# One change to a long-convolution, gate and ELU-MLP kernel: the filter's four steps taken from four groups in each slot, and two subtractions of the first part moved to GpSimd

## The chip, the cores and the metric

The kernel runs on one core of a Trainium2 chip. The metric is the device time of one execution in microseconds (us). Three runs of the kernel before gave 3637.33 us as their median (3637.32 to 3637.77). About 0.2% (7 us) is what a measurement of this kernel can tell from no change.

## The reference

Two stages, all in float32. The first gates two inputs, convolves the product along the sequence (12480 long, by a Fourier transform of twice that length) with a filter that a small MLP makes from position embeddings, and gates the result again. The second is an MLP with ELU.

```python
B, S, D = 4, 12480, 128                       # x, v: (4, 12480, 128); pos_emb: (12480, 64)
h_mlp  = np.maximum(pos_emb @ w1, 0.0) @ w2   # w1 64x64, w2 64x128
h_filt = h_mlp * np.exp(-0.01 * pos)[:, None]
u  = x * v
Uf = np.fft.rfft(u, n=2 * S, axis=1)
Hf = np.fft.rfft(h_filt, n=2 * S, axis=0)
y  = np.fft.irfft(Uf * Hf[None], n=2 * S, axis=1)[:, :S]
a  = (x * y).reshape(B * S, D)
h  = a @ w_in                                 # w_in 128x2048, float64 in DRAM
g  = np.where(h > 0, h, np.exp(np.minimum(h, 0)) - 1)
out = g @ w_out                               # w_out 2048x128, float64 in DRAM
```

## The kernel before

The transform is split in two: 104 x 60 positions per half of the sequence. Stage 1 does transforms of length 104 as matmuls, stage 2 the ones of length 60, the product with the filter's spectrum and the first half of the way back. The rest of the way back and the MLP run block by block. A float32 operand of a large matmul is split in a rounded high part (`_h`) and a rest (`_l`, the subtraction), and `mm3` multiplies them in three matmuls (lines 53, 54, 55).

The program has three parts. The **first part** is stage 1 of batch 0 together with the filter and the conversion of the MLP's weights (`first=True`). The second is stage 2 of batch 0. The third is the MLP of all batches, with the stages of batches 1 to 3 beside it. Only the first part is touched. Its order is written out by hand: each engine executes its instructions in the order in which the code issues them, and SyncE issues all the large DMAs in that order.

The first part runs over 15 groups `g` of 4 columns of 60. For each group x and v are loaded (`xt`, `vt`), gated (`vt = xt * vt`, line 102, on GpSimd from group 2 on), split (`u_h` on ScalarE, line 110, `u_l` on VectorE, line 111) and transformed in four pieces `i`, each an `mm3` of 512 columns into `aps`. Two pieces are a **slot** `q = 2g + r`, the pieces of a slot being `w = 0` and `w = 1`; there are 30 slots. The output `a_sb` is copied from PSUM by VectorE for `w = 0` (line 153) and by ScalarE for `w = 1`, and stored to `a_d`.

In slot q the filter's group q + 1 (of 30) is also made, in four steps: `step(q+1, 0)` transposes four tiles of `pos` into `pt` (line 217) and ScalarE copies them to `pt_sb`; `step(q+1, 1)` multiplies by `w1` into `rp` (line 223), and ScalarE writes the ReLU `r_sb` (line 225); `step(q+1, 2)` multiplies by `w2` into `hps` (line 231), VectorE multiplies by the window into `h_sb` (line 234), ScalarE writes `h_h`, and VectorE the rest `h_l` (line 242); `transform(q)` then multiplies the group made in the slot before by the transform matrix into `Hps` (12 matmuls of 256 columns), ScalarE and VectorE write `hsb` from it (VectorE at line 256), and it is stored to `h_d`. `pt`, `rp` and `hps` share one pool of two PSUM banks.

In each of the first 16 slots one of 16 chunks of the MLP's weights is also converted from float64: ten VectorE instructions (`weights`, lines 290 to 307), and in the slot after that `split_w`, which copies the high part (`wi_h`, `wo_h`, ScalarE) and subtracts on GpSimd (`wi_l`, `wo_l`, line 318).

Of the kernel before, what the change touches and what calls it, by code (L numbers as in the profile page):

```python
# [38 lines left out]
def fftconv_gate_elu_mlp_kernel(ctx: ExitStack, tc: tile.TileContext, x, v, pos_emb, w1, w2,  # L39
# [41 lines left out]
    def stage1(st, h, ps_pool, ps_tag, first):  # L81
# [22 lines left out]
        def split(g):  # L104
            if g >= NG:
                return
            vt = ld.pop(g)[1]
            u_h = up.tile([N1, 2, G, D], F32R, tag="u_h", name="u_h")
            u_l = up.tile([N1, 2, G, D], F32R, tag="u_l", name="u_l")
            copy(u_h, vt)  # L110
            nc.vector.tensor_tensor(out=u_l, in0=vt, in1=u_h, op=ALU.subtract)
            us[g] = (u_h, u_l)

        def store():
# [4 lines left out]

        if first:  # L120
            filt = Filter(st)
            for g in range(4):
                filt.load(g)
                if g < 3:
                    load(g)
                filt.load_w(g)
            gate(0)
            gate(1)
            for q in range(3):
                filt.step(0, q)  # L130
        else:
            load(0)
            load(1)
            gate(0)
            gate(1)
        split(0)
        for g in range(NG):
            if first:
                gate(g + 2)
            u_h, u_l = us.pop(g)  # L140
            for i in range(4):
                r, w = divmod(i, 2)
                f = FWD[w][r]
                if w == 0:
                    a_sb = ap.tile([N1, G, Z, 2, D], F32 if first else F32R, tag="a_sb", name="a_sb")
                if first:
                    q = 2 * g + r
                    filt.step(q + 1, 2 * w)
                ps = ps_pool.tile([N1, 512], F32, tag=ps_tag, name="aps")
                mm3(ps, dft_h[:, f, :], dft_l[:, f, :], u_h[:, w], u_l[:, w])  # L150
                src = ps.rearrange("p (n d) -> p n d", n=G)
                if first and w == 0:
                    nc.vector.tensor_copy(out=a_sb[:, :, 0, w], in_=src)
                else:
                    copy(a_sb[:, :, 0, w], src)
                if not first:
                    nc.vector.tensor_tensor(out=a_sb[:, :, 1, w], in0=src, in1=a_sb[:, :, 0, w], op=ALU.subtract)
                if first:
                    if w == 0:
                        filt.step(q + 1, 1)  # L160
                        filt.load(q + 4)
                        filt.load_w(q + 4)
                    else:
                        filt.transform(q)
                        filt.weights(q)
                        filt.split_w(q - 1)
# [12 lines left out]
        if first:
            filt.flush()  # L180


    class Filter:
# [2 lines left out]

        def __init__(self, st):
            c1 = st.enter_context(tc.tile_pool(name="c1", bufs=1))
            self.pp = st.enter_context(tc.tile_pool(name="pp", bufs=5))
            self.hp = st.enter_context(tc.tile_pool(name="hp", bufs=1))  # L190
            self.wl = st.enter_context(tc.tile_pool(name="wl", bufs=1))
            self.psh = st.enter_context(tc.tile_pool(name="psh", bufs=2, space=PS))
            self.psH = st.enter_context(tc.tile_pool(name="psH", bufs=1, space=PS))
            self.w1 = c1.tile([64, 64], F32, name="w1_sb")
            self.w2 = c1.tile([64, D], F32, name="w2_sb")
            self.win = c1.tile([N1, 2, N2], F32, name="win_sb")
            nc.scalar.dma_start(out=self.w1, in_=w1)
# [11 lines left out]
        def step(self, g, q):  # L209
# [2 lines left out]
            hp, psh = self.hp, self.psh  # L212
            if q == 0:
                p = self.pos.pop(g)
                pt = psh.tile([64, 2 * GF, N1], F32, tag="h", name="pt")
                for n in range(2 * GF):
                    nc.tensor.transpose(out=pt[:, n, :], in_=p[:, n // GF, n % GF, :], identity=id_sb[:N1, :N1])
                pt_sb = hp.tile([64, 2 * GF, N1], F32, tag="pt_sb", name="pt_sb")
                copy(pt_sb, pt)
                self.t[g] = pt_sb  # L220
            elif q == 1:
                rp = psh.tile([64, 2 * GF, N1], F32, tag="h", name="rp")
                nc.tensor.matmul(out=rp, lhsT=self.w1, rhs=self.t[g], start=True, stop=True)
                r_sb = hp.tile([64, 2 * GF, N1], F32, tag="r_sb", name="r_sb")
                nc.scalar.activation(out=r_sb, in_=rp, func=ACTF.Relu)
                self.t[g] = r_sb
            elif q == 2:
                r_sb = self.t.pop(g)
                hps = psh.tile([N1, 2, GF, D], F32, tag="h", name="hps")
                for n in range(2 * GF):  # L230
                    nc.tensor.matmul(out=hps[:, n // GF, n % GF, :], lhsT=r_sb[:, n, :], rhs=self.w2,
                                     start=True, stop=True)
                h_sb = hp.tile([N1, 2, GF, D], F32, tag="h_sb", name="h_sb")
                nc.vector.tensor_tensor(
                    out=h_sb, in0=hps,
                    in1=self.win[:, :, g * GF:(g + 1) * GF].rearrange("p w (n o) -> p w n o", o=1).to_broadcast([N1, 2, GF, D]),
                    op=ALU.mult)
                h_h = hp.tile([N1, 2, GF * D], F32R, tag="h_h", name="h_h", bufs=2)
                h_l = hp.tile([N1, 2, GF * D], F32R, tag="h_l", name="h_l", bufs=2)
                hv = h_sb.rearrange("p w n d -> p w (n d)")  # L240
                copy(h_h, hv)
                nc.vector.tensor_tensor(out=h_l, in0=hv, in1=h_h, op=ALU.subtract)
                self.hs[g] = (h_h, h_l)

        def transform(self, g):
# [21 lines left out]
        def load_w(self, i):  # L267
# [1 line left out]
            if i >= self.NW:  # L269
                return  # L270
            m, c = divmod(i, DFF // WC)
            z = self.wl.tile([128, WC, 2], U32, tag="z", name="z", bufs=5)
# [385 lines left out]
    with ExitStack() as st:  # L658
# [3 lines left out]
        nc.scalar.dma_start(out=id_sb, in_=ident)  # L662
        copy(dft_h, dft_sb)
        nc.vector.tensor_tensor(out=dft_l, in0=dft_sb, in1=dft_h, op=ALU.subtract)
        psa = st.enter_context(tc.tile_pool(name="psa", bufs=4, space=PS))
        for _ in stage1(st, 0, psa, "a", True):
            pass
    with ExitStack() as st:
# [68 lines left out]
```

## Time and profile before

| what | value |
|---|---|
| median of 3 runs | 3637.33 us |
| the profiled execution: time / span of its trace | 3646.31 us / 3644.5 us |
| TensorE busy, whole span | 3434.0 us (94%) |
| VectorE / ScalarE / GpSimd busy, whole span | 3136.5 / 2418.3 / 2276.2 us |
| mean granted TensorE clock, whole span | 0.967 |
| first part, end of the first `Hps` to end of the last | 29.4 to 271.9 us |
| in that stretch: TensorE / VectorE / ScalarE / GpSimd busy | 211.2 / 143.1 / 94.2 / 75.7 of 242.6 us |

The profiled execution is 9 us (0.25%) longer than the median of the runs. Busy times are those of the hardware profiler; a matmul's end is modelled and lies some tenths of a microsecond behind the start of the one that follows, so starts are compared with starts. The granted clock is a share of 2.4 GHz; 0.50 is 1.2 GHz.

### The profile page before, as it was taken

To read this page: it belongs to the slowest core of one execution; us is meant where nothing else is said; L and a number is where in the kernel's file an instruction comes from. 1 tells how busy PE (TensorE), PEld (TensorE's weight loads), DVE (VectorE), ACT (ScalarE), POOL (GpSimd) and SP (SyncE) were. 2 spreads that over 40 slices of the span, in tenths; PEclk is the share of its full clock that TensorE was granted. 3 is DMA by queue.
4 is the path that set the end of the run, shared out by engine and by line. 5 is a ranking of instruction groups with operands and counts; after the bars stand their busy time and mean duration, and the time that the engine had idled before them with its cause. 6 is when DMAs were issued, how large, how long until landed. Compare 5 with 4: busy or idle time off the path is not lost.

```text
span 3644.5 us, 53113 instructions
## 1 busy us (share of the span) xinstructions
PE 3434.0 (94%) x18444; PEld 3158.4 (87%) x18444; DVE 3136.5 (86%) x3941; ACT 2418.3 (66%) x3290; POOL 2276.2 (62%) x1578
## 2 busy tenths in 40 slices
PE   7887878989999999989999999989999999999999
PEld 5666767879998998879999998879999999999998
DVE  5647988989999988989999988979999988888887
ACT  3334546866666677866666677866666677777776
POOL 3406875857777765557766756657666655655555
PEclk8769998999999999999999999999999999999999
DMA  6648886767777735778888846778888832222220
GB/s 186 185 127 241 267 242 194 222 181 201 203 205 208 201 109 165 242 202 220 238 221 229 227 114 185 241 199 225 233 228 232 237 88 60 59 66 60 69 59 24
DMA packets 383995, 646.29 MB, mean 177 GB/s; under 512 B 24679, under 2 KB 170439, under 8 KB 374367
## 3 DMA queue, kind: packets, MB, share of 16 engines
q1 hardware_dynamic: 383305, 642.73, 62.4%
q8 instruction: 146, 2.39, 0.3%
q14 instruction: 123, 1.00, 0.1%
q10 hardware_dynamic: 421, 0.16, 0.0%
HBM read 412.76 MB, written 230.03 MB: 176 GB/s over the span
## 4 chain that ended last, share of the span: by engine, by line
PE 76%; DVE 8%; ACT 4%; DMA 4%; issue 4%; POOL 3%; SPq 0%; POOLq 0%; DVEq 0%; ACTq 0%
PE fps L53 9%; PE fps L55 9%; PE fps L54 9%; PE ops L53 9%; PE ops L54 9%; PE ops L55 8%; PE bps L439 4%; DVE g_l L567 2%; PE xps L53 2%; PE xps L54 2%; PE xps L55 2%; PE yps L53 2%; PE yps L54 2%; PE yps L55 2%; PE otp L589 1%
## 5 line engine op out<-in xcount | busy, mean ns | idle before, releaser
L561 POOL CAST g_h<-g 128x832 fp32r<-128x832 f32 x960 | 1232.5, 1286 | 1051.3 <-DVE g L558 1050.5
L551 ACT ACTIVATE n<-fps 128x832 f32<-128x832 f32 x960 | 831.9, 867 | 723.1 <-PE fps L55 704.2
L558 DVE SCALAR_TENSOR_TENSOR g<-n,fps 128x832 f32<-128x832 f32 x960 | 975.9, 1017 | 258.5 <-ACT n L552 253.0
L567 DVE TENSOR_TENSOR g_l<-g,g_h 128x832 fp32r<-128x832 f32 x960 | 1097.7, 1143 | 9.3 <-POOL g_h L561 9.3
L552 ACT ACTIVATE n<-n 128x832 f32<-128x832 f32 x960 | 864.4, 900 | 30.5
L53 PE MATMUL fps<-t_h,wi_h 128*128 128x416 f32 x1920 | 716.4, 373 | 0.7 <-ACT t_h L58 0.7
L54 PE MATMUL ops<-g_l,wo_h 128*128 128x416 f32 x1920 | 680.9, 355 | 23.6 <-DVE g_l L567 23.2
L53 PE MATMUL ops<-g_h,wo_h 128*128 128x416 f32 x1920 | 680.4, 354 | 4.7
L55 PE MATMUL fps<-t_h,wi_l 128*128 128x416 f32 x1920 | 677.0, 353 | 0.0
L54 PE MATMUL fps<-t_l,wi_h 128*128 128x416 f32 x1920 | 676.7, 352 | 0.0
L55 PE MATMUL ops<-g_h,wo_l 128*128 128x416 f32 x1920 | 675.1, 352 | 0.0
L420 POOL TENSOR_TENSOR p<-p 120x768 f32<-120x768 f32 x204 | 480.9, 2357 | 69.2 <-DVE p L414 49.3
L54 PEld LDWEIGHTS ops<-g_l,wo_h 128*128 128x128 f32 x1920 | 362.3, 189 | 45.8 <-DVE g_l L567 41.1
L53 PEld LDWEIGHTS fps<-t_h,wi_h 128*128 128x128 f32 x1920 | 364.2, 190 | 21.3 <-ACT t_h L58 1.0
L53 PEld LDWEIGHTS ops<-g_h,wo_h 128*128 128x128 f32 x1920 | 361.6, 188 | 20.0 <-issue 17.5
L54 PEld LDWEIGHTS fps<-t_l,wi_h 128*128 128x128 f32 x1920 | 365.8, 191 | 15.0 <-DVE t_l L540 0.3
L55 PEld LDWEIGHTS fps<-t_h,wi_l 128*128 128x128 f32 x1920 | 362.7, 189 | 2.8
L55 PEld LDWEIGHTS ops<-g_h,wo_l 128*128 128x128 f32 x1920 | 361.5, 188 | 3.4
L412 DVE TENSOR_TENSOR p<-xps,f 120x512 f32<-120x512 f32 x416 | 283.4, 681 | 24.9 <-DMA f<-f_d 14.7
L421 POOL TENSOR_TENSOR p<-p 120x256 f32<-120x256 f32 x204 | 246.0, 1206 | 16.0
L439 PE MATMUL bps<-p,t 120*120 120x256 f32 x832 | 219.1, 385 | 31.5 <-POOL p L421 26.6
L347 DVE TENSOR_TENSOR tl<-t,th 120x360 fp32r<-120x360 f32 x208 | 202.1, 971 | 44.9 <-ACT th L58 31.4
(95 smaller groups left out, 4979.0 us busy)
## 6 DMA issues: line engine op xcount, KB each, us to landing
a_d<-a_sb SPq DMA_DIRECT2D x90, 832.0 KB
al<-a_d SPq DMA_DIRECT2D x156, 480.0 KB
f<-f_d SPq DMA_DIRECT2D x312, 240.0 KB
b_d<-b_sb SPq DMA_DIRECT2D x156, 480.0 KB
b<-b_d SPq DMA_DIRECT2D x90, 832.0 KB
t<-in_tab_dram SPq DMA_DIRECT2D x208, 281.2 KB
xt<-in_x_dram SPq DMA_DIRECT2D x60, 416.0 KB
vt<-in_v_dram SPq DMA_DIRECT2D x60, 416.0 KB
```

Source lines behind the costliest of these rows:

```text
L53: nc.tensor.matmul(out=ps, lhsT=hi, rhs=bh, start=start, stop=False)
L54: nc.tensor.matmul(out=ps, lhsT=hi, rhs=bl, start=False, stop=False)
L55: nc.tensor.matmul(out=ps, lhsT=lo, rhs=bh, start=False, stop=stop)
L412: nc.vector.tensor_tensor(out=p[:, :, :2], in0=ps[:, :, 0:1, :].to_broadcast([RI, TG, 2, D]), in1=f[:, :, r], op=ALU.mult)
L420: e.tensor_tensor(out=q, in0=q, in1=p, op=ALU.add)
L421: e.tensor_tensor(out=q[:, :, 1], in0=q[:, :, 1], in1=q[:, :, 2], op=ALU.add)
L439: nc.tensor.matmul(out=ps[:, o], lhsT=t[:, o, 3 * N2:], rhs=y[:, o, :2], start=True, stop=True)
L551: nc.scalar.activation(out=n, in_=ps[:, :, :NT], func=ACTF.Relu, scale=-1.0)
L552: nc.scalar.activation(out=n, in_=n, func=ACTF.Exp, scale=-1.0)
L558: nc.vector.scalar_tensor_tensor(out=g, in0=n, scalar=-1.0, in1=ps[:, :, :NT], op0=ALU.add, op1=ALU.max)
L561: nc.gpsimd.tensor_copy(out=g_h, in_=g)
L567: nc.vector.tensor_tensor(out=g_l, in0=g, in1=g_h, op=ALU.subtract)
```

## The change

In slot q the filter's steps are now taken from four different groups: `step(q+3, 0)`, then the first piece's `aps`, `step(q+1, 2)`, `step(q+2, 1)`, the second piece's `aps` and `transform(q)`. What a step needs was issued in an earlier slot. Before the first slot the first steps of the groups 0 to 2 are issued. `pt`, `rp` and `hps` have a PSUM bank each, `aps` has three banks instead of four, and the SBUF tiles between the steps have two buffers. The conversion of the weights' chunks is spread: one in each of the slots 0, 1 and 2 and then one in every second slot up to 28. The subtractions `u_l` (from group 1 on) and `h_l` go from VectorE to GpSimd.

```diff
@@ stage1, split and the start
-            nc.vector.tensor_tensor(out=u_l, in0=vt, in1=u_h, op=ALU.subtract)
+            e = nc.gpsimd if first and g else nc.vector
+            e.tensor_tensor(out=u_l, in0=vt, in1=u_h, op=ALU.subtract)
...
-            for g in range(4):
+            for g in range(5):
                 filt.load(g)
                 if g < 3:
                     load(g)
                 filt.load_w(g)
             gate(0)
+            for q in range(3):
+                for i in range(3 - q):
+                    filt.step(i, q)
             gate(1)
-            for q in range(3):
-                filt.step(0, q)
@@ stage1, the slots
                 if first:
                     q = 2 * g + r
-                    filt.step(q + 1, 2 * w)
+                    filt.step(q + 3 - w, w)
...
                     if w == 0:
-                        filt.step(q + 1, 1)
-                        filt.load(q + 4)
-                        filt.load_w(q + 4)
+                        filt.step(q + 1, 2)
+                        filt.load(q + 5)
                     else:
                         filt.transform(q)
-                        filt.weights(q)
-                        filt.split_w(q - 1)
+                        if q % 2 == 0 or q == 1:
+                            c = (q + 1) // 2 + (q > 1)
+                            filt.load_w(c + 5)
+                            filt.weights(c)
+                            filt.split_w(c - 1)
@@ Filter
-            self.psh = st.enter_context(tc.tile_pool(name="psh", bufs=2, space=PS))
+            self.psh = st.enter_context(tc.tile_pool(name="psh", bufs=1, space=PS))
...
-                pt = psh.tile([64, 2 * GF, N1], F32, tag="h", name="pt")
+                pt = psh.tile([64, 2 * GF, N1], F32, tag="t", name="pt")
...
-                rp = psh.tile([64, 2 * GF, N1], F32, tag="h", name="rp")
+                rp = psh.tile([64, 2 * GF, N1], F32, tag="r", name="rp")
...
-                nc.vector.tensor_tensor(out=h_l, in0=hv, in1=h_h, op=ALU.subtract)
+                nc.gpsimd.tensor_tensor(out=h_l, in0=hv, in1=h_h, op=ALU.subtract)
@@ the first part's PSUM
-        psa = st.enter_context(tc.tile_pool(name="psa", bufs=4, space=PS))
+        psa = st.enter_context(tc.tile_pool(name="psa", bufs=3, space=PS))
```

Left out here: `pt_sb`, `r_sb` and `h_sb` get two buffers, `pos` and `z` six instead of five, and the last `split_w` follows the last slot.

TensorE, from one `transform` to the next (one slot, `Hps` left out), the rows of before with - and of the change with +:

```order
-L217 MATMUL pt<-id_sb,pos 64x104 x4
-L53 MATMUL aps<-u_h,dft_h 104x512
-L54 MATMUL aps<-u_l,dft_h 104x512
-L55 MATMUL aps<-u_h,dft_l 104x512
-L223 MATMUL rp<-pt_sb,w_sb 64x416
-L231 MATMUL hps<-w_sb,r_sb 104x128 x4
+L222 MATMUL pt<-id_sb,pos 64x104 x4
+L53 MATMUL aps<-u_h,dft_h 104x512
+L54 MATMUL aps<-u_l,dft_h 104x512
+L55 MATMUL aps<-u_h,dft_l 104x512
+L236 MATMUL hps<-w_sb,r_sb 104x128 x4
+L228 MATMUL rp<-pt_sb,w_sb 64x416
```

`rp` and `hps` have changed places; before, `rp` reads the `pt` of its own slot and `hps` the `rp` just before it, now `rp` reads the `pt` of the slot before, and `hps` the `rp` of the slot before.

TensorE at the start of the program, before:

```order
L217 MATMUL pt<-id_sb,pos 64x104 x4
L223 MATMUL rp<-pt_sb,w_sb 64x416
L231 MATMUL hps<-w_sb,r_sb 104x128 x4
L217 MATMUL pt<-id_sb,pos 64x104 x4
L53 MATMUL aps<-u_h,dft_h 104x512
```

and with the change:

```order
L222 MATMUL pt<-id_sb,pos 64x104 x12
L228 MATMUL rp<-pt_sb,w_sb 64x416 x2
L236 MATMUL hps<-w_sb,r_sb 104x128 x4
L222 MATMUL pt<-id_sb,pos 64x104 x4
L53 MATMUL aps<-u_h,dft_h 104x512
```

Three groups of transposes instead of one and two `rp` instead of one now stand ahead of the first `hps`.

GpSimd in the first part, before, where the chunks go over from w_in to w_out:

```order
L102 TENSOR_TENSOR vt<-xt,vt 104x1024
L318 TENSOR_TENSOR wi_l<-r,wi_h 128x256
L318 TENSOR_TENSOR wo_l<-r,wo_h 128x256
L102 TENSOR_TENSOR vt<-xt,vt 104x1024
L318 TENSOR_TENSOR wo_l<-r,wo_h 128x256 x2
```

and with the change, over one group (two slots):

```order
L102 TENSOR_TENSOR vt<-xt,vt 104x1024
L247 TENSOR_TENSOR h_l<-h_sb,h_h 104x512
L323 TENSOR_TENSOR wi_l<-r,wi_h 128x256
L112 TENSOR_TENSOR u_l<-vt,u_h 104x1024
L247 TENSOR_TENSOR h_l<-h_sb,h_h 104x512
L102 TENSOR_TENSOR vt<-xt,vt 104x1024
```

A group has one gating, one weight subtraction, one `u_l` and two `h_l` there, and `u_l` stands behind the weight subtraction.

## Rows read from the trace of the kernel before

**Rows 1.** Stretches: us, busy PE, PEld, DVE, ACT, POOL; clock; DMA share; GB/s.

```profile
29.40:271.97 242.57, 211.16 (x915) 155.17 (x912) 143.09 (x288) 94.20 (x172) 75.70 (x28) 0.73 0.55 162
209.00:250.00 41.00, 38.49 (x129) 26.88 (x128) 13.96 (x19) 12.72 (x22) 2.38 (x1) 0.50 0.40 112
252.00:271.00 19.00, 16.26 (x99) 12.08 (x100) 9.25 (x13) 8.96 (x16) 0.00 (x0) 1.00 0.48 131
340.00:500.00 160.00, 143.37 (x809) 123.19 (x808) 146.49 (x201) 87.90 (x170) 130.62 (x133) 1.00 0.88 267
46.00:50.00 4.00, 1.90 (x8) 0.78 (x7) 3.90 (x13) 2.36 (x5) 3.01 (x1) 0.97 0.80 280
50.00:56.00 6.00, 6.00 (x26) 5.29 (x25) 2.99 (x5) 1.82 (x4) 0.00 (x0) 0.50 0.71 245
```

**Rows 2.** Waits until 280 us: who, for whom; us in total, times, longest.

```profile
PE hps L231 <- ACT r_sb L225: 18.0, 30, 0.6
PE rp L223 <- ACT pt_sb L58: 14.1, 13, 1.5
```

**Rows 3.** Last `Hps` matmul of slots 0, 1 and 29: start, duration.

```profile
29.00 0.40 PE L55 MATMUL Hps<-h_h,dft_l 104*104 104x256 f32 x1
...
38.65 0.42 PE L55 MATMUL Hps<-h_h,dft_l 104*104 104x256 f32 x1
...
271.66 0.28 PE L55 MATMUL Hps<-h_h,dft_l 104*104 104x256 f32 x1
```

**Rows 4.** TensorE in one slot at full clock, in order of time.

```profile
262.69 0.52 PE L217 MATMUL pt<-id_sb,pos 104*64 104x104 f32 x4
262.98 0.46 PE L53 MATMUL aps<-u_h,dft_h 104*104 104x512 f32 x1
...
263.94 0.91 PE L223 MATMUL rp<-pt_sb,w_sb 64*64 64x416 f32 x2
265.44 1.12 PE L231 MATMUL hps<-w_sb,r_sb 64*104 64x128 f32 x8 [0.60 <-ACT r_sb L225]
266.49 0.48 PE L53 MATMUL aps<-u_h,dft_h 104*104 104x512 f32 x1
...
267.27 0.28 PE L53 MATMUL Hps<-h_h,dft_h 104*104 104x256 f32 x1
...
268.69 0.40 PE L53 MATMUL aps<-u_h,dft_h 104*104 104x512 f32 x1
```

**Rows 5.** A slot with weights, behind its `Hps`: ScalarE and GpSimd.

```profile
114.55 0.60 ACT L58 ACTIVATE hsb<-Hps 104x512 f32<-104x512 f32 x1 [1.36 <-PE Hps L55]
...
115.04 0.41 ACT L58 ACTIVATE wo_h<-r 128x256 fp32r<-128x256 f32 x1
...
115.35 1.05 ACT L58 ACTIVATE u_h<-vt 104x1024 fp32r<-104x1024 f32 x1
115.53 3.00 POOL L318 TENSOR_TENSOR wo_l<-r,wo_h 128x256 fp32r<-128x256 f32 x1 [2.45 <-ACT wo_h L58]
```

**Rows 6.** GpSimd's operations by line: ns min/median/max, first and last start.

```profile
L318 POOL TENSOR_TENSOR wo_l<-r,wo_h x8: 723/3004/3007, 107.5 to 166.2; 128x256 fp32r<-128x256 f32 x8
...
L515 POOL TENSOR_TENSOR b<-b,b x28: 2386/2406/3432, 579.1 to 1343.2; 104x1024 fp32r<-104x1024 f32 x28
...
L102 POOL TENSOR_TENSOR vt<-xt,vt x58: 2333/2436/3816, 20.9 to 2386.5; 104x1024 f32<-104x1024 f32 x58
```

**Rows 7.** DMA of the first 280 us, all queues.

```profile
DMA packets 27703, 47.20 MB, mean 169 GB/s; under 512 B 2096, under 2 KB 10622, under 8 KB 27688
```

**Rows 8.** The start, in order of time.

```profile
13.04 2.03 PE L231 MATMUL hps<-w_sb,r_sb 64*104 64x128 f32 x8 [0.60 <-ACT r_sb L225]
...
15.18 1.23 DVE L102 TENSOR_TENSOR vt<-xt,vt 104x1024 f32<-104x1024 f32 x1 [4.76 <-DMA vt<-in_v_dram]
...
18.64 1.23 DVE L111 TENSOR_TENSOR u_l<-vt,u_h 104x1024 fp32r<-104x1024 f32 x1 [0.25 <-ACT u_h L58]
...
20.86 2.34 POOL L102 TENSOR_TENSOR vt<-xt,vt 104x1024 f32<-104x1024 f32 x1 [20.42 <-DMA vt<-in_v_dram]
```

More of the change, by code (lines that the diff above doesn't have):

```diff
@@ L179, in stage1 @@
         if first:
+            filt.split_w(filt.NW - 1)
             filt.flush()
@@ L188, in __init__ @@
             c1 = st.enter_context(tc.tile_pool(name="c1", bufs=1))
-            self.pp = st.enter_context(tc.tile_pool(name="pp", bufs=5))
+            self.pp = st.enter_context(tc.tile_pool(name="pp", bufs=6))
             self.hp = st.enter_context(tc.tile_pool(name="hp", bufs=1))
             self.wl = st.enter_context(tc.tile_pool(name="wl", bufs=1))
-            self.psh = st.enter_context(tc.tile_pool(name="psh", bufs=2, space=PS))
+            self.psh = st.enter_context(tc.tile_pool(name="psh", bufs=1, space=PS))
             self.psH = st.enter_context(tc.tile_pool(name="psH", bufs=1, space=PS))
@@ L214, in step @@
                 p = self.pos.pop(g)
-                pt = psh.tile([64, 2 * GF, N1], F32, tag="h", name="pt")
+                pt = psh.tile([64, 2 * GF, N1], F32, tag="t", name="pt")
                 for n in range(2 * GF):
                     nc.tensor.transpose(out=pt[:, n, :], in_=p[:, n // GF, n % GF, :], identity=id_sb[:N1, :N1])
-                pt_sb = hp.tile([64, 2 * GF, N1], F32, tag="pt_sb", name="pt_sb")
+                pt_sb = hp.tile([64, 2 * GF, N1], F32, tag="pt_sb", name="pt_sb", bufs=2)
                 copy(pt_sb, pt)
@@ L221, in step @@
             elif q == 1:
-                rp = psh.tile([64, 2 * GF, N1], F32, tag="h", name="rp")
+                rp = psh.tile([64, 2 * GF, N1], F32, tag="r", name="rp")
                 nc.tensor.matmul(out=rp, lhsT=self.w1, rhs=self.t[g], start=True, stop=True)
-                r_sb = hp.tile([64, 2 * GF, N1], F32, tag="r_sb", name="r_sb")
+                r_sb = hp.tile([64, 2 * GF, N1], F32, tag="r_sb", name="r_sb", bufs=2)
                 nc.scalar.activation(out=r_sb, in_=rp, func=ACTF.Relu)
@@ L232, in step @@
                                      start=True, stop=True)
-                h_sb = hp.tile([N1, 2, GF, D], F32, tag="h_sb", name="h_sb")
+                h_sb = hp.tile([N1, 2, GF, D], F32, tag="h_sb", name="h_sb", bufs=2)
                 nc.vector.tensor_tensor(
@@ L271, in load_w @@
             m, c = divmod(i, DFF // WC)
-            z = self.wl.tile([128, WC, 2], U32, tag="z", name="z", bufs=5)
+            z = self.wl.tile([128, WC, 2], U32, tag="z", name="z", bufs=6)
             if m == 0:
```

## The prediction

> **What bounds the kernel now.** First I read busy time by stretches, then the waits, then single slots in order of time. The first part, from the end of slot 0's `Hps` (29.00 + 0.40 = 29.40 us) to that of slot 29 (271.66 + 0.28 = 271.94 us), takes 242.5 us [rows 1, 3]. TensorE is the busiest engine there, 211 of 243 us, but at a mean granted clock of 0.73; VectorE has 143, ScalarE 94 and GpSimd 76 us [rows 1]. From the end of slot 1 (38.65 + 0.42 = 39.07 us) on, a slot is (271.94 - 39.07) / 28 = 8.32 us [rows 3]. The reader is to see two losses in it. One is the chain inside a slot: TensorE stands 14.1 us for `pt_sb` before `rp` and 18.0 us for `r_sb` before `hps`, about 1.1 us a slot [rows 2]. The other is the clock that these waits lead to. In 46 to 50 us TensorE was busy for 1.90 of 4.00 us, and then it ran 50 to 56 us at 0.50 without a gap, which costs 3 us of full-clock work [rows 1]. In 209 to 250 us it stood at 0.50 although it was busy for 38.5 of 41 us; in 252 to 271 us, where no weights are converted, it kept 1.00 [rows 1].
>
> **A slot at full clock.** From start to start: `pt` 0.29, `aps` 0.78 twice, `hps` 1.05, `Hps` 1.42, and `rp` by its busy time, 0.91; the sum is 5.23 us. The slot that these come from is 268.69 - 262.69 = 6.00 us, so 0.77 us of it is the chain [rows 4].
>
> **Part 1: steps of four groups.** All instructions of TensorE stay. `rp` now reads a `pt_sb` and `hps` an `r_sb` of the slot before, so both waits go; what hides ScalarE's copies is a slot of TensorE's own work. Saved at full clock: 0.77 us a slot. Saved on top: the clock, if TensorE has no long gaps any more. That is the larger sum, since 5.23 us against the measured 8.32 us is 3.1 us a slot.
>
> **What is late next.** Call E the end of the `Hps` of an even slot. By the rows of such a slot ScalarE starts `hsb` 0.04 us after E (114.55 is E + 0.04), then the weights' copy, then `u_h`, which ends at 115.35 + 1.05 = E + 1.89. The weight subtraction starts on GpSimd at E + 1.02 and takes 3.00 us, because VectorE's conversion runs beside it, so GpSimd is free for `u_l` at E + 4.02 [rows 5]; alone the same subtraction took 0.72 us [rows 6].
>
> **Part 2: subtractions on GpSimd.** `u_l` is 104x1024 there. The nearest row is the same subtraction of the third part on GpSimd, median 2.41 us (2.39 to 3.43) [rows 6], against 1.23 us on VectorE [rows 8]. With 2.41 us it is done at E + 6.43. TensorE has 5.23 us of the odd slot and 0.29 us of `pt` to do meanwhile, and the first `aps` matmul needs only `u_h` (a third of 0.78 us), so it gets to the matmul that reads `u_l` at E + 5.78 and waits 0.65 us a group. Behind that stand 0.52 + 1.05 + 0.91 + 0.78 + 1.42 = 4.68 us [rows 4]; the next E comes after 6.43 + 4.68 = 11.1 us, and a slot is 5.55 us. Queued behind `u_l` on GpSimd are two `h_l` and the gating of a later group. `h_l` has no row: 256 columns took 0.72 us and 1024 took 2.41 us, these are the bounds; on the line between them 512 columns take 1.28 us, which I take. A group's GpSimd work is then 2.44 (gating) + 2.41 + 3.00 + 2 x 1.28 = 10.4 us [rows 5, 6], 0.7 us under the 11.1 us, so it just fits. VectorE is relieved and has room: it is busy for 143 of 243 us now [rows 1].
>
> The Trainium skill ("GPSIMD Engine Reference", section 4.1) says that an elementwise operation with two inputs is about twice as slow on GpSimd and belongs on VectorE. The trace agrees with the ratio (2.41 against 1.23 us). By that rule the move is a loss; it becomes one only where GpSimd sets the slot, which is the second rival below.
>
> **Part 3: DMA.** The first 280 us moved 47.2 MB, nearly all of it the first part's [rows 7]: about 45 MB, 3.0 MB a group. In 11.1 us that is 270 GB/s. The longest dense stretch of the trace, 340 to 500 us, moved 267 GB/s at a DMA share of 0.88 with TensorE 90% busy [rows 1]. So the DMA will be at about what this trace has shown it to do, and some of its delays will reach the engines. I take 0.25 us a slot for this and for a clock that falls now and then (one fall of 3 us in six groups alone would be that much): 5.8 us a slot, at which the DMA has 259 GB/s. For this friction the bounds are 0 and 1.5 us (a fall of 3 us in every group).
>
> The Trainium skill ("DMA: Bandwidth & Descriptors", section "Where 436 GB/s comes from") puts the limit of transfers to or from HBM at about 358 GB/s for a core. An estimate from that figure: 3.0 MB would take 8.4 us, the DMA would not be felt, and the slot would stay at 5.55 us, 7 us less in all. No stretch in the rows here shows such a rate.
>
> **Part 4: start, banks, weights.** At the start three `pt` and two `rp` now stand ahead of the first `hps`. The third `pt` needs `pos` of group 2, which is issued between group 1's v (landed 15.18 us) and group 2's (20.86 us) [rows 8]; by its place among these bytes, a third of the way, 16.9 us. At low clock `hps` takes 2.03 us [rows 8], and I double the full-clock times of the rest [rows 4]: `pt` 0.6, two `rp` with an `r_sb` copy between (their bank is single) 4.2, `hps` 2.0, then about 3.5 us for `h_sb`, `h_h`, `u_h` and `u_l` (1.23 us) in turn. `u_l` of group 0 is then done at about 27.2 us instead of 18.64 + 1.23 = 19.87 us [rows 8]. Slot 0 behind it has no waits any more, so its end is late by about 6 us, not 7.3 us; I put the end of slot 1 at 44 us against 39.07 us. The single banks cost nothing as long as the copies keep up: `pt_sb` follows `u_h` at E + 1.89, the next `pt` comes at E + 5.23; were that cover gone, a wait as long as the 0.60 us of an `hsb` copy [rows 5] in each slot would cost 17 us. The weights' chunks, spread over the part, are loaded five ahead, so their place behind the `h_d` store on SyncE's queue is hidden. The last slots have no `pt`, `rp` or `hps` any more: about 3 us less. What comes after the first part is unchanged.
>
> **The sum.** 44 + 28 x 5.8 - 3 = 203.4 us for the end of the last `Hps`, against 271.9 us: 68.5 us less. From the profiled execution's 3646.3 us that leaves 3578 us; this execution was 9 us above the median of the runs, and from 3637.3 us it is 3569 us.
>
> **The rivals.**
> - TensorE alone is the bound, nothing waits: 5.23 us a slot, end at 187 us, 3553 us. For it: 0.65 us of wait a group is little. Against it: GpSimd and the DMA are as full as TensorE.
> - GpSimd is the bound. With the longest of each row (3.43, 3.82, 3.01 and two `h_l` of 2.41 us [rows 6]) a group is 15.1 us, a slot 7.5 us, the end at 251 us, 3616 us. For it: these operations stretch from 0.72 to 3.00 us beside VectorE's conversion. Against it: the medians add up to 10.4 us, and VectorE converts in one slot of two only.
> - The clock falls in every group. 3 us a group on top of 11.1 us: 7.05 us a slot, end at 238 us, 3604 us. For it: the fall after 46 to 50 us. Against it: in 252 to 271 us TensorE was busy for 16.3 of 19 us and kept 1.00 [rows 1]; now it has smaller gaps.
> - Slower: TensorE stays at 0.50. Then a slot is 2 x 5.23 = 10.5 us, the end at 334 us, 3699 us. It decides from the point where slots are above (271.9 - 41) / 28 = 8.25 us. For it: 209 to 250 us, 94% busy and still 0.50. Against it: that stretch still had both waits, and slots of the changed order have none at low clock.
> - The change does not do what it says: with one bank each, the steps wait for one another as before, and the time stays at 3637 us. Against it: the reader of each bank runs more than half a slot ahead of its next writer.
>
> **How the numbers follow.** The forecast (50 to 82 us less, 3555 to 3587 us) has a chance of 0.53, TensorE alone 0.12, GpSimd 0.10, the clock 0.18, slower 0.04, no effect 0.03. The range 3552 to 3612 us leaves out the last two, half of GpSimd's and some of the first rival's. Faster by over 0.2% (7 us, about what a measurement of this kernel can tell from no change) is all but the last two: 0.93; within 0.2% 0.03; slower 0.04.
>
> **What would show it.** Right: `rp` and `hps` no longer wait for `pt_sb` and `r_sb`; the granted clock of the first part is above 0.9; slots of 5.5 to 6 us; TensorE's largest wait is for `u_l` on GpSimd; the first `u_l` ends at 25 to 28 us; the DMA rate is near 260 GB/s. Wrong: a clock under 0.8, GpSimd busy for nearly the whole part with waits for `h_l`, or waits for `vt`'s load in GpSimd's column. An end of the last `Hps` after 230 us would make the forecast wrong even with the mechanism right.

## The result, and the profile after

| | us |
|---|---|
| before, median of 4 runs | 3637.55 (3637.32 to 3641.95) |
| after, median of 4 runs | 3592.60 (3591.93 to 3593.52) |
| ratio, 95% interval | 0.9874 [0.9857, 0.9891] |
| predicted | 3569, range 3552 to 3612 |
| profiled execution of after: time / span | 3593.21 / 3591.4 |

The change makes the kernel 45 us (1.2%) faster. The sign and the range were right; the forecast gain of 68.5 us was too large by 24 us, and the time lies outside the forecast's own band (50 to 82 us less, 3555 to 3587 us). Of all executions behind the times of this document one, of e3_weights_early below, was slow (4173 us at a mean granted clock of 0.75): it is left out of that kernel's ratio, but not of its median (3565.24 us; 3563.96 without it).

First the ends of slots 0, 1 and 29, the last `Hps` matmul of each in order of time (start, duration):

```profile
36.00 0.41 PE L55 MATMUL Hps<-h_h,dft_l 104*104 104x256 f32 x1
...
42.02 0.28 PE L55 MATMUL Hps<-h_h,dft_l 104*104 104x256 f32 x1
...
221.01 0.28 PE L55 MATMUL Hps<-h_h,dft_l 104*104 104x256 f32 x1
```

Against [rows 3] the first part ends at 221.29 us instead of 271.94, 50.65 us earlier. The spans differ by 3644.5 - 3591.4 = 53.1 us, so nearly all of the gain lies in this part. It starts later (36.41 us for the end of slot 0 against 29.40) and runs faster: from the end of slot 1 a slot takes (221.29 - 42.30) / 28 = 6.39 us against 8.32.

The stretches of after, with the columns of [rows 1]; the first is the whole part, the second is nearly free of falls of the clock, the third is one of five stretches at 0.50:

```profile
36.41:221.30 184.89, 169.78 (x905) 121.07 (x902) 103.25 (x244) 87.05 (x168) 143.74 (x69) 0.89 0.68 210
80.00:100.00 20.00, 18.30 (x107) 12.36 (x106) 12.94 (x32) 9.77 (x20) 18.83 (x9) 0.98 0.83 268
99.20:106.00 6.80, 6.80 (x25) 4.81 (x23) 1.89 (x6) 3.46 (x7) 3.45 (x3) 0.50 0.80 247
```

The five begin at 58, 99, 137, 164 and 215 us and take 10.4, 6.8, 6.8, 14 and 3.6 us. The clock rose from 0.73 to 0.89, and with it the DMA rate from 162 to 210 GB/s; GpSimd went from 76 of 243 to 144 of 185 us. The waits of TensorE until 240 us (us in total, times, longest):

```profile
PE aps L54 <- POOL u_l L112: 9.8, 11, 2.0
PE hps L236 <- ACT r_sb L230: 5.3, 3, 2.3
```

The 14.1 us of `rp` for `pt_sb` in [rows 2] are gone, the 18.0 us of `hps` for `r_sb` have become 5.3, and `u_l` is the new and largest wait. One slot at full clock, TensorE in order of time, with the `u_l` on GpSimd that it waits for:

```profile
187.19 2.56 POOL L112 TENSOR_TENSOR u_l<-vt,u_h 104x1024 fp32r<-104x1024 f32 x1
...
188.20 0.52 PE L222 MATMUL pt<-id_sb,pos 104*64 104x104 f32 x4
188.50 0.46 PE L53 MATMUL aps<-u_h,dft_h 104*104 104x512 f32 x1
...
189.79 0.48 PE L54 MATMUL aps<-u_l,dft_h 104*104 104x512 f32 x1 [0.84 <-POOL u_l L112]
...
194.50 0.52 PE L222 MATMUL pt<-id_sb,pos 104*64 104x104 f32 x4
...
199.71 0.52 PE L222 MATMUL pt<-id_sb,pos 104*64 104x104 f32 x4
```

This slot takes 6.30 us, the next 5.21, together 11.51 us or 5.76 a slot; in [rows 4] a slot at full clock took 6.00 us and still had the `r_sb` wait. The slot with weights, VectorE and GpSimd behind its `Hps`, to be laid beside [rows 5]:

```profile
195.73 3.02 POOL L323 TENSOR_TENSOR wo_l<-r,wo_h 128x256 fp32r<-128x256 f32 x1 [1.04 <-ACT wo_h L58]
...
195.98 0.28 DVE L295 TENSOR_SCALAR k<-z 128x256 uint32<-128x256 uint32 x1
...
198.18 0.84 DVE L312 TENSOR_TENSOR r<-r,k 128x256 f32<-128x256 f32 x1
...
198.71 2.56 POOL L112 TENSOR_TENSOR u_l<-vt,u_h 104x1024 fp32r<-104x1024 f32 x1
```

`wo_l` takes 3.02 us, as in [rows 5], and `u_l` starts directly behind it. The first and the last of the ten conversion operations are shown (195.98 and 198.18). `wo_l` starts 0.25 us ahead of the first and ends at 198.75; alone it takes 0.73 us (e3_weights_early below), so it seems to have been held until about 198.02, when nine of the ten had started: not by one operation but by a run of them. The last one, `r<-r,k`, in turn takes 0.84 us instead of 0.42 and ends 0.27 us behind `wo_l`. GpSimd by line until 240 us (busy us, mean ns of one | idle before), where [rows 6] had the bounds:

```profile
L247 POOL TENSOR_TENSOR h_l<-h_sb,h_h 104x512 fp32r<-104x512 f32 x30 | 38.6, 1285 | 41.9 <-ACT h_h L58 41.2
L102 POOL TENSOR_TENSOR vt<-xt,vt 104x1024 f32<-104x1024 f32 x13 | 31.8, 2446 | 0.0
```

The gating never waits for its load (its idle time is 0.0), so its loads set no slot. At the start, against [rows 8], the first `hps` comes at 21.44 instead of 13.04 us and the first `u_l` is done at 27.55 instead of 19.87:

```profile
21.44 2.03 PE L236 MATMUL hps<-w_sb,r_sb 64*104 64x128 f32 x8
...
25.84 1.71 DVE L112 TENSOR_TENSOR u_l<-vt,u_h 104x1024 fp32r<-104x1024 f32 x1 [0.51 <-ACT u_h L58]
```

Last, a place where the chain breaks, VectorE, GpSimd and TensorE in order of time:

```profile
130.57 2.57 POOL L112 TENSOR_TENSOR u_l<-vt,u_h 104x1024 fp32r<-104x1024 f32 x1
130.81 2.61 DVE L311 TENSOR_TENSOR k<-k,s 128x256 uint32<-128x256 uint32 x1
133.45 0.42 DVE L312 TENSOR_TENSOR r<-r,k 128x256 f32<-128x256 f32 x1
134.40 0.68 DVE L239 TENSOR_TENSOR h_sb<-hps,win_sb 104x512 f32<-104x512 f32 x1
135.11 0.63 ACT L58 ACTIVATE h_h<-h_sb 104x512 fp32r<-104x512 f32 x1 [5.59 <-DVE h_sb L239]
135.65 0.49 ACT L230 ACTIVATE r_sb<-rp 64x416 f32<-64x416 f32 x1
136.19 1.60 PE L236 MATMUL hps<-w_sb,r_sb 64*104 64x128 f32 x8 [2.30 <-ACT r_sb L230]
```

VectorE's `k<-k,s` takes 2.61 us, where the `r<-r,k` of the same size behind it takes 0.42. It starts 0.24 us after GpSimd's `u_l`; it ends at 133.42, 0.28 us after `u_l` (133.14). `h_sb`, `h_h` and `r_sb` are queued behind it one after the other, and TensorE loses 2.30 us. This pair of operations is what the experiments turn on.

### The profile page after: what moved, and what is told of

Its sections match the earlier page's. It is cut to its first block, busy times and chain, and to the rows that moved or that the text cites. A ratio compares the mean times of both kernels' runs of the same rounds, so it can differ in the third digit from the quotient of the medians.

```text
span 3591.4 us, 53160 instructions
## 1 busy us (share of the span) xinstructions
PE 3393.5 (94%) x18444; PEld 3120.6 (87%) x18444; DVE 3098.7 (86%) x3897; ACT 2413.0 (67%) x3290; POOL 2353.6 (66%) x1622
## 4 chain that ended last, share of the span: by engine, by line
PE 77%; DVE 8%; POOL 4%; issue 4%; DMA 3%; ACT 3%; SPq 0%; POOLq 0%; DVEq 0%; ACTq 0%
PE fps L53 9%; PE fps L55 9%; PE fps L54 9%; PE ops L53 9%; PE ops L54 9%; PE ops L55 9%; PE bps L444 4%; DVE g_l L572 2%; PE xps L53 2%; PE xps L54 2%; PE xps L55 2%; PE yps L53 2%; PE yps L54 2%; PE yps L55 2%; PE otp L594 1%
## 5 line engine op out<-in xcount | busy, mean ns | idle before, releaser
L54 PE MATMUL ops<-g_l,wo_h 128*128 128x416 f32 x1920 | 679.9, 354 | 24.1 <-DVE g_l L572 23.6
L417 DVE TENSOR_TENSOR p<-xps,f 120x512 f32<-120x512 f32 x416 | 283.6, 682 | 23.6 <-DMA f<-f_d 9.6
```

What stands on the lines that cost most here:

```text
L54: nc.tensor.matmul(out=ps, lhsT=hi, rhs=bl, start=False, stop=False)
L417: nc.vector.tensor_tensor(out=p[:, :, :2], in0=ps[:, :, 0:1, :].to_broadcast([RI, TG, 2, D]), in1=f[:, :, r], op=ALU.mult)
```

## The experiments

Three theories stood at the beginning. Mine: the order (Part 1) brings the gain, the subtractions on GpSimd (Part 2) are neutral, and what is missing from the forecast is a clock that falls more often than assumed. Two rivals: the DMA, then near its highest rate, holds the part back; or the gain is the relief of VectorE and not the order. Each kernel was timed beside runs of the kernel before on the same chip, and each ratio is to those.

| kernel | us, median | ratio to before, 95% interval | end of the first part | granted clock from slot 1 on |
|---|---|---|---|---|
| before (profiled) | | | 271.9 | 0.73 |
| after | 3592.60 | 0.9874 [0.9857, 0.9891] | 221.3 | 0.89 |
| e1_order_only | 3637.70 | 1.0005 [0.9995, 1.0015] | 263.7 | 0.78 |
| e2_subtractions_only | 3637.59 | 0.9992 [0.9979, 1.0005] | 265.0 | 0.77 |
| e8_h_l_only | 3595.73 | 0.9889 [0.9866, 0.9912] | 225.2 | 0.88 |
| e7_u_l_only | 3587.93 | 0.9864 [0.9835, 0.9893] | 220.2 | 0.87 |
| e11_split_late | 3598.89 | 0.9905 [0.9873, 0.9937] | 226.5 | 0.88 |
| e6_fill | 3585.59 | 0.9856 [0.9828, 0.9885] | 210.7 | 0.97 |
| e5_swap | 3618.93 | 0.9948 [0.9928, 0.9968] | 252.0 | 0.74 |
| e3_weights_early | 3565.24 | 0.9806 [0.9787, 0.9826] | 193.7 | 0.95 |
| e9_spread | 3556.63 | 0.9779 [0.9757, 0.9800] | 185.5 | 1.00 |
| e10_start | 3547.08 | 0.9764 [0.9727, 0.9801] | 176.5 | 1.00 |

Ends and clocks are those of the one profiled execution of each kernel. The intervals of e3_weights_early, e9_spread and e10_start overlap from one to the next; that each is faster than the one before rests on the ends of the first part and on executions that do not overlap (3563.9 to 3566.5, 3555.9 to 3558.5, 3546.1 to 3549.7 us), though on different chips.

**The two halves apart.** First the subtractions alone, in the order of before:

```diff
-            nc.vector.tensor_tensor(out=u_l, in0=vt, in1=u_h, op=ALU.subtract)
+            e = nc.gpsimd if first and g else nc.vector
+            e.tensor_tensor(out=u_l, in0=vt, in1=u_h, op=ALU.subtract)
...
-                nc.vector.tensor_tensor(out=h_l, in0=hv, in1=h_h, op=ALU.subtract)
+                nc.gpsimd.tensor_tensor(out=h_l, in0=hv, in1=h_h, op=ALU.subtract)
```

> The kernel before with only the two subtractions moved to GpSimd. Theory (the gain comes from the order): the waits for pt_sb and r_sb inside the slot stay and with them the low clock; 3625 to 3640 us. Rival 2 (relief of VectorE): most of the 45 us gain, 3592 to 3610 us.

Nothing gained, as the theory said. The waits inside a slot are those of before (30 to 275 us):

```profile
PE hps L232 <- ACT r_sb L226: 16.8, 28, 0.6
PE rp L224 <- ACT pt_sb L58: 16.5, 19, 1.5
```

Then the order alone, which is the change with both subtractions left on VectorE:

```diff
-            e = nc.gpsimd if first and g else nc.vector
-            e.tensor_tensor(out=u_l, in0=vt, in1=u_h, op=ALU.subtract)
+            nc.vector.tensor_tensor(out=u_l, in0=vt, in1=u_h, op=ALU.subtract)
...
-                nc.gpsimd.tensor_tensor(out=h_l, in0=hv, in1=h_h, op=ALU.subtract)
+                nc.vector.tensor_tensor(out=h_l, in0=hv, in1=h_h, op=ALU.subtract)
```

> The changed order of the steps, with both subtractions (u_l, h_l) back on VectorE. Theory (a slot of the changed kernel is set by a chain of engines behind VectorE's weight conversion, and by the falls of the clock that its wait brings): the wait for u_l goes, but u_l and h_l now delay h_sb, h_h and r_sb on VectorE and ScalarE. Counted from the end of Hps, r_sb is ready after about 7.7 us and hps wants it after 6.3 us, so hps waits some 1.4 us a group where u_l's wait was about 1 us; 5.95 us a slot beside 5.78 us: 3592 to 3610 us. Rival 1 (the DMA sets the slot): the bytes are the same, the time stays within 3 us of the changed kernel's 3592.6 us. Rival 2 (the gain came from the relief of VectorE, not from the order): back to 3625 to 3637 us.

Nothing gained either, so the first half of my theory fell: neither part does anything by itself, both together are worth 45 us. The rival that VectorE's relief is the gain had named 3625 to 3637 us here, but e2_subtractions_only gave that relief in the old order, without gain. The waits of TensorE from 30 to 225 us have a new one beside that for `r_sb` (15.8 us, 11 times):

```profile
PE aps L54 <- DVE u_l L111: 10.6, 8, 1.9
```

The timeline of one group shows where it comes from, GpSimd, VectorE and TensorE in order of time:

```profile
102.64 3.02 POOL L322 TENSOR_TENSOR wi_l<-r,wi_h 128x256 fp32r<-128x256 f32 x1 [12.22 <-ACT wi_h L58]
...
105.62 2.56 POOL L102 TENSOR_TENSOR vt<-xt,vt 104x1024 f32<-104x1024 f32 x1
...
105.86 3.40 DVE L111 TENSOR_TENSOR u_l<-vt,u_h 104x1024 fp32r<-104x1024 f32 x1
...
109.32 0.48 PE L54 MATMUL aps<-u_l,dft_h 104*104 104x512 f32 x1 [1.52 <-DVE u_l L111]
```

The gating stands directly behind the weight subtraction on GpSimd and starts 0.24 us ahead of `u_l`. `u_l` takes 3.40 us instead of 1.23 [rows 8] and ends at 109.26, 1.08 us after the gating (108.18): it ran only when GpSimd was through. TensorE waits 1.52 us for it. The Trainium skill ("SBUF — State Buffer", section "Who interferes with whom") says that a VectorE instruction with two inputs in SBUF contends with a GpSimd instruction that reads SBUF, and that whichever issues first has the shared pair of ports for its whole length while the other is fully blocked. The trace agrees to 0.15 us: held until 108.18 us, 1.22 us of work would end at 109.40, and `u_l` ended at 109.26. `wo_l` of after does not fit the part on who issues first: by the profile it starts ahead of the run of conversion operations (and while VectorE's `hsb` operation runs, 195.38 to 196.07 us), and still it is the one that waits; why, no run shows.

**Which subtraction matters.** `h_l` alone moved, `u_l` on VectorE:

```diff
-            e = nc.gpsimd if first and g else nc.vector
-            e.tensor_tensor(out=u_l, in0=vt, in1=u_h, op=ALU.subtract)
+            nc.vector.tensor_tensor(out=u_l, in0=vt, in1=u_h, op=ALU.subtract)
```

> The changed kernel with u_l back on VectorE, h_l on GpSimd. Theory (u_l on VectorE is what costs the gain): waits for u_l and for r_sb of 1 to 1.6 us each in a group as with the order alone; 3625 to 3640 us. Rival (h_l matters as much): 3600 to 3620 us.

It gained nearly all, against my expectation: both ranges missed. Beside taking work from VectorE, `h_l` now stands on GpSimd between the weight subtraction and the gating, and waits there for `h_h`:

```profile
117.89 3.04 POOL L322 TENSOR_TENSOR wi_l<-r,wi_h 128x256 fp32r<-128x256 f32 x1 [1.86 <-ACT wi_h L58]
...
121.14 1.21 DVE L111 TENSOR_TENSOR u_l<-vt,u_h 104x1024 fp32r<-104x1024 f32 x1
...
124.28 1.26 POOL L246 TENSOR_TENSOR h_l<-h_sb,h_h 104x512 fp32r<-104x512 f32 x1 [3.35 <-ACT h_h L58]
...
125.51 2.37 POOL L102 TENSOR_TENSOR vt<-xt,vt 104x1024 f32<-104x1024 f32 x1
```

So the gating comes late, `u_l` has the port to itself and takes 1.21 us. TensorE's wait for `u_l` falls from 10.6 us in 8 to 0.5 us in one (30 to 225 us); the one for `r_sb` stays (18.2 us, 14 times). So does the meeting of the weight subtraction with the conversion (3.04 us here): neither of these is what the order alone loses by. What the wait for `r_sb` is made of shows behind the rows above:

```profile
123.58 0.63 ACT L58 ACTIVATE h_h<-h_sb 104x512 fp32r<-104x512 f32 x1 [4.42 <-DVE h_sb L238]
...
124.66 1.12 PE L235 MATMUL hps<-w_sb,r_sb 64*104 64x128 f32 x8 [1.40 <-ACT r_sb L229]
```

`r_sb` stands behind `h_h` on ScalarE, and `h_h` waits for `h_sb`, which stands on VectorE behind the conversion, `u_l` and `a_sb`. That is the chain, and the 1.4 us, that the expectation of e1_order_only had worked out. The other half, `u_l` on GpSimd and `h_l` back on VectorE:

```diff
-                nc.gpsimd.tensor_tensor(out=h_l, in0=hv, in1=h_h, op=ALU.subtract)
+                nc.vector.tensor_tensor(out=h_l, in0=hv, in1=h_h, op=ALU.subtract)
```

> The changed kernel with h_l back on VectorE, u_l on GpSimd. Theory (in the run with the order alone it was u_l on VectorE, 3.40 us beside GpSimd's gating instead of 1.22 us, that cost the gain; h_l is not on the chain): 3588 to 3605 us. Rival (both moves are needed): 3620 to 3640 us.

It gained as much as the whole change (the intervals overlap); there the gating and `u_l` are on one engine and cannot meet. From these two I formed the new theory: what the order alone loses is the meeting of the gating with `u_l`, and either subtraction on GpSimd removes it. Its test leaves both subtractions on VectorE and moves the weight's split, ScalarE's copy and GpSimd's subtraction, into the following half slot (against e1_order_only):

```diff
                     if w == 0:
                         filt.step(q + 1, 2)
                         filt.load(q + 5)
+                        if q == 2 or (q > 2 and q % 2):
+                            filt.split_w(0 if q == 2 else q // 2)
...
                             filt.weights(c)
-                            filt.split_w(c - 1)
```

> The order alone (both subtractions on VectorE, 3637.7 us) with the weight's split, ScalarE's copy and GpSimd's subtraction, moved from behind its conversion to the first half of the following slot. My theory now: the order alone loses because GpSimd's gating stands directly behind the weight subtraction and so runs beside u_l on VectorE, where u_l took 3.40 us; with the subtraction later, GpSimd's gating comes at another moment, u_l takes about 1.2 us and the time is 3590 to 3610 us with both subtractions on VectorE. Rival: VectorE has simply too much to do for the shorter slot, wherever GpSimd's work stands; then the time stays at 3630 to 3640 us. A third outcome that fits the theory, not the rival: the gating, without the weight ahead of it, starts sooner and runs beside the conversion instead; then conversion rows of about 2.5 us show in the trace in place of the 3.40 us of u_l.

```profile
108.89 1.22 DVE L111 TENSOR_TENSOR u_l<-vt,u_h 104x1024 fp32r<-104x1024 f32 x1
...
112.42 0.92 POOL L323 TENSOR_TENSOR wi_l<-r,wi_h 128x256 fp32r<-128x256 f32 x1 [10.30 <-ACT wi_h L58]
...
113.30 2.35 POOL L102 TENSOR_TENSOR vt<-xt,vt 104x1024 f32<-104x1024 f32 x1
```

3598.9 us, as the theory said: `u_l` is back at 1.22 us, `wi_l` at 0.92 instead of 3.02, and the order alone, with both subtractions on VectorE, is worth 1% (its interval overlaps that of the change). VectorE did not have too much to do for the gain; it was held up.

**What the remaining wait costs.** Five matmuls in the place of one fill the wait for `u_l` in each group; four of them are extra work:

```diff
+                if first and g and i == 0:
+                    for _ in range(4):
+                        nc.tensor.matmul(out=ps, lhsT=dft_h[:, f, :], rhs=u_h[:, w], start=True, stop=True)
```

> The changed kernel with four more matmuls in the place where TensorE waits for u_l: the first aps matmul of each group from 1 on is done five times (the first four results are overwritten), 4 x 0.23 us at full clock, about as much as the wait of 0.85 us. Theory (the wait costs most by the falls of the clock that it brings): the work is more, but fewer stretches at 0.50; of the 42 us at low clock a half goes, 3575 to 3588 us. Rival (only the wait itself costs): no gain, 3592 to 3600 us.

By its time alone this is not told from the change: 0.9856 [0.9828, 0.9885] against 0.9874 [0.9857, 0.9891]. The trace is clearer. Its first part has two stretches at low clock in place of five (one of them below), and ends 10.6 us earlier although TensorE has more to do:

```profile
61.60:65.20 3.60, 3.60 (x20) 3.30 (x18) 0.00 (x0) 1.62 (x4) 1.77 (x2) 0.55 0.74 212
80.00:120.00 40.00, 40.00 (x238) 28.48 (x237) 23.31 (x54) 20.84 (x41) 36.55 (x19) 1.00 0.82 268
```

**Which of GpSimd's operations goes first.** `u_l` ahead of the weight subtraction, so that TensorE should get it sooner:

```diff
                             filt.weights(c)
-                            filt.split_w(c - 1)
...
                     split(g + 1)
+                if first and w == 1 and (q % 2 == 0 or q == 1):
+                    filt.split_w(c - 1)
```

> The changed kernel with u_l ahead of the weight subtraction on GpSimd. Theory (it is VectorE's conversion that holds GpSimd, whatever instruction is there): u_l starts 1.9 us after the end of Hps, is held until the conversion ends and is ready after about 6.4 us as before; 3588 to 3597 us. Rival 3 (u_l is late because the weight subtraction is queued ahead of it): u_l is ready about 4.4 us after the end of Hps, the wait goes; 3565 to 3582 us.

Both expectations missed: it is 26 us slower than the change. GpSimd, VectorE and TensorE in order of time:

```profile
67.91 4.03 POOL L112 TENSOR_TENSOR u_l<-vt,u_h 104x1024 fp32r<-104x1024 f32 x1 [1.11 <-ACT u_h L58]
...
69.72 2.50 DVE L313 TENSOR_TENSOR r<-r,k 128x256 f32<-128x256 f32 x1
...
74.53 2.03 PE L237 MATMUL hps<-w_sb,r_sb 64*104 64x128 f32 x8 [1.83 <-ACT r_sb L231]
```

`u_l` now meets VectorE's conversion, takes 4.03 us, and then holds up `r<-r,k` (0.42 us by itself) until 72.22, 0.28 us after its own end at 71.94. `h_sb` and `r_sb` follow late, as at 136 us of after, and TensorE stops. It is the same lock, met from the other side.

**The meeting moved.** The conversion `weights` moved to the first half of the slot, where GpSimd has no weight subtraction and no `u_l`, but an `h_l`; the splits stay (against the change):

```diff
                         filt.load(q + 5)
+                        if q % 2 == 0 or q == 1:
+                            filt.weights((q + 1) // 2 + (q > 1))
...
-                            filt.weights(c)
                             filt.split_w(c - 1)
```

> The changed kernel with VectorE's conversion of a weights' chunk moved half a slot forward, behind h_sb of the even slot, so that it is over when GpSimd does the weight subtraction and u_l. Theory (GpSimd is held by VectorE's conversion, so u_l is late): the weight subtraction takes 0.72 us instead of 3.0 us, u_l is ready about 4.5 us after the end of Hps, the wait of 0.85 us at aps goes, the slot is 5.2 to 5.4 us, and the clock falls less often; 3560 to 3578 us. Rival 1 (the DMA sets the slot): 3.0 MB in 10.5 us would be 286 GB/s, more than the trace has shown over a long stretch; 3587 to 3594 us.

3565 us. The weight subtraction is at 0.73 us in the median and `u_l` at 2.38 (ns min/median/max below), the wait for `u_l` is gone, and from 80 to 160 us TensorE is never idle at full clock, while the DMA moves 284 GB/s in the first half (shown) and 288 in the second:

```profile
L324 POOL TENSOR_TENSOR wi_l<-r,wi_h x8: 725/730/836, 42.7 to 118.6; 128x256 fp32r<-128x256 f32 x8
```

```profile
80.00:120.00 40.00, 40.00 (x249) 29.20 (x248) 28.47 (x64) 23.81 (x46) 34.78 (x21) 1.00 0.86 284
46.80:60.40 13.60, 12.96 (x49) 10.08 (x50) 7.83 (x16) 5.86 (x11) 9.25 (x5) 0.51 0.62 169
```

The DMA rival falls with this: more than the 270 GB/s of the prediction is carried beside a TensorE without gaps. The two engines still meet, at another place:

```profile
105.53 2.48 POOL L248 TENSOR_TENSOR h_l<-h_sb,h_h 104x512 fp32r<-104x512 f32 x1 [0.90 <-ACT h_h L58]
...
106.90 1.39 DVE L313 TENSOR_TENSOR r<-r,k 128x256 f32<-128x256 f32 x1
```

`h_l` takes 2.48 us where 1.28 is its own time, and `r<-r,k` 1.39 where 0.42 is, ending 0.28 us behind `h_l`. From 80 to 160 us TensorE waits for neither, so the meeting costs it nothing there: what the move took away is not the lock but its place on the chain to TensorE.

One stretch at low clock is left, 46.8 to 60.4 us, behind the slots 1 and 2, which both convert a chunk. So one chunk is converted in every two slots from the start (against e3_weights_early, shortened):

```diff
-                        if q % 2 == 0 or q == 1:
-                            filt.weights((q + 1) // 2 + (q > 1))
+                        if q % 2 == 0 or q == 29:
+                            filt.weights((q + 1) // 2)
```

> The kernel with the conversion half a slot forward (the run of 3565 us), and the chunks in every second slot from the first on, the last in slot 29, none in slot 1. Theory (TensorE's wait of 1.93 us at 47 us came from conversions in slots 0, 1 and 2 in a row, and brought the stretch at 0.50 from 46.8 to 60.4 us): that stretch goes, some 7 us less; 3555 to 3561 us. Rival (the clock falls there anyway, with the start of the program): 3563 to 3567 us.

3556.6 us; from 40 to 180 us TensorE is never idle and keeps its full clock (two windows of it below):

```profile
40.00:80.00 40.00, 40.00 (x252) 29.47 (x250) 27.96 (x63) 23.83 (x47) 34.48 (x20) 1.00 0.86 278
140.00:180.00 40.00, 40.00 (x245) 29.21 (x245) 27.89 (x61) 23.09 (x45) 30.34 (x18) 1.00 0.72 229
```

Before 36 us the clock's column is no guide: it reads 1.00 from 28 us on as well, but slot 0's `Hps` matmuls take 0.41 us each there, as at half clock, against 0.28 us later.

**The start.** What was left is the first 36 us. The loads of `pos`, x and v go ahead of the weights' first tile, and group 0 is split before the filter's steps (against e9_spread, shortened):

```diff
             gate(0)
-            for q in range(3):
-                for i in range(3 - q):
-                    filt.step(i, q)
+            filt.step(0, 0)
+            split(0)
+            filt.step(1, 0)
+            filt.step(0, 1)
...
-        split(0)
+        if not first:
+            split(0)
```

> The spread-out weights (3556.6 us) with another prologue: the positions of the first groups, the first xt and vt are loaded ahead of the weights' first tile, the split of group 0 stands right behind its gating, and the filter's first steps are taken in the order that their operands arrive. What is left of the first part's loss by now lies in its start: the first Hps ends at 36 us there, of which the TensorE work of the prologue is some 5 us. My theory: the prologue waits for u_l of group 0 (ready at 27 us only because its split stands behind the filter's steps), so the first Hps comes some 8 to 10 us sooner and the time is 3545 to 3550 us. Rival: the loads decide, since the same bytes have to land first; then the time is 3553 to 3558 us.

```profile
11.33 1.22 DVE L112 TENSOR_TENSOR u_l<-vt,u_h 104x1024 fp32r<-104x1024 f32 x1 [1.12 <-ACT u_h L58]
```

The first `u_l` is done at 12.55 us instead of 27.55, the first part ends 9 us earlier (176.5 against 185.5), and the kernel takes 3547.1 us: 2.4% under before and the best here. The cost of the start in Part 4 was real, and it was a matter of order, not of bytes; which of the two orders gave it, that of the loads or that of the steps, is not taken apart.

## Why the prediction was right in sign and too large

Point by point, by the forecast's own terms for the end of the first part, 44 + 28 x 5.8 - 3 = 203.4 us against 221.3 measured, 17.9 us too early:

- **Start:** 44 us for the end of slot 1; measured 42.30. The first `u_l` was put at 27.2 us and came at 27.55. Right, 1.7 us to the good. (A third of the way from 15.18 to 20.86 us is 17.1, not 16.9: nothing hangs on it.)
- **A slot without disturbance:** 5.23 us of TensorE and 0.65 us of wait in a group made 5.55 us. Measured 5.76: the slot without a wait takes 5.21 us, and the one with it 1.09 more, of which the trace puts 0.84 down to `u_l`. That 0.84 counts from a modelled end; by starts the wait is 0.99, since the matmul that reads `u_l` comes 1.29 us behind the one ahead of it (188.50 to 189.79) where it comes 0.30 behind it in the slot without a wait. `u_l` took 2.56 us instead of 2.41, and the interpolated `h_l` 1.285 instead of 1.28.
- **Friction, 0.25 us a slot: this is the step that failed.** It stood for the DMA and for a clock that falls "now and then", one fall of 3 us in six groups. No trace shows a part of the DMA in it. The falls are larger: five stretches, 41.6 us at 0.50, which hold 20.8 us of full-clock work, so they cost about 20.8 us. By subtraction they cost 221.3 - 42.3 + 3 - 28 x 5.76 = 20.7 us; so close an agreement is luck, since the 3 us of the last slots were not measured and not every group has the full wait. That is 0.74 us a slot; the upper bound in the text was 1.5 us, and the rival of a fall in every group would have been 3604 us. The time lies between this rival and the forecast. With e6_fill the wait was filled and three of the five stretches went; with e9_spread the waits went and so did all of them from the end of slot 0 to the end of the first part.
- **What the falls followed:** waits of 2.04, 0.85, 2.30, 0.85 and 1.55 us. Only two of them have about the size that was worked out (0.65); the 2.30 is the break of the chain through VectorE at 136 us, a mechanism that no term had. Not every wait of such a size was followed by a fall: `hps` waited 1.35 and 1.61 us for `r_sb` at 44.70 and 51.60 us, and `aps` between 0.75 and 0.85 us five more times, with no stretch at 0.50 in the five microseconds behind any of them.
- **From the part to the kernel:** 68.5 us was taken from the median, 9 us below the profiled execution, as if these 9 us lay outside the first part, which no trace shows. The profiled executions differ by 3646.3 - 3593.2 = 53.1 us, the medians by 45. Of the 23.6 us by which the forecast was off, this is the second piece, 53.1 - 44.9 = 8.2 us; what lies behind the first part gave back 53.1 - 50.65 = 2.5 us (17.9 + 8.2 - 2.5 = 23.6).
- **The credit given to the parts was wrong.** The text put the gain down to Part 1 and called Part 2 a move that "just fits" because VectorE "has room". e1_order_only shows Part 1 alone at no gain, e11_split_late shows it at 1% with the same operations on VectorE. What Part 2 does is to keep the gating away from `u_l`. The prediction had seen that a GpSimd subtraction stretches from 0.72 to 3.00 us beside VectorE [rows 5, 6], but it priced it on GpSimd only and did not ask what it does to VectorE's operation. That the time fell in the range is in so far luck: the order that the text relied on gains nothing without a pairing whose reason it had not seen.
- **The marks named in advance:** no wait for `pt_sb`, `u_l` as the largest wait and the first `u_l` between 25 and 28 us came. Slots of 5.5 to 6 us (5.76) and a DMA rate near 260 GB/s (268) came only where the clock was full; over the part they are 6.39 us and 210 GB/s. `hps` still waits for `r_sb` three times. A clock above 0.9 did not quite come (0.89), and its shortfall is the missing time.

What stays open: why the first of the following two waits of after led to no fall of the clock, and the second to the stretch from 99.2 us on:

```profile
85.47 0.48 PE L54 MATMUL aps<-u_l,dft_h 104*104 104x512 f32 x1 [0.84 <-POOL u_l L112]
...
97.03 0.48 PE L54 MATMUL aps<-u_l,dft_h 104*104 104x512 f32 x1 [0.85 <-POOL u_l L112]
```

Open too is why `wo_l`, which starts ahead of the run of conversion operations, is held until the run is nearly over, while `u_l` at 130.57 us holds VectorE up.

## What to carry to other kernels

Before an operation is moved between VectorE and GpSimd, lay the two engines' timelines side by side and look which two-input operations start within a few tenths of a microsecond of one another: the later one takes its own time plus what is left of the earlier one, and what is queued behind it pays; a GpSimd operation beside a run of VectorE's back to back can wait for nearly all of them. Such a meeting is removed by order (a half slot later, another operation in between) as well as by changing the engine, and one whose results nobody waits for may stay (`h_l` in e3_weights_early). And where TensorE's clock is in play, a wait of one microsecond is to be priced with the stretch at half clock that can follow it, from the profile's own rows.

## What the runs showed of the hardware

- An operation that is blocked at the shared port shows as busy, not as waiting: 3.40 us for 1.22 us of work (`u_l` on VectorE), 2.61 and 2.50 for 0.42 (conversion), 4.03 for 2.38 (`u_l` on GpSimd), 3.02 for 0.73 (`wo_l`). The profile names no releaser for it; one sees it only by an operation whose time differs from its twin's.
- A blocked VectorE operation ended 0.28 us (three times, 0.42 us of work) and 1.08 us (1.22 us of work) after GpSimd's, so the two ran one after the other, not at half speed.
- A DMA rate of 284 GB/s beside TensorE that is busy for 40.0 of 40 us did not slow a slot, although 267 GB/s was the highest that the trace of before had shown in a long stretch.
